# State products in four narrow column tiles, placed between the past products

## The chip, the cores and the metric

The kernel runs on one core of a Trainium2 chip. The metric is the time of one execution on the device, in microseconds (us): the median of three runs is 507.63 (507.57 to 507.75).

## The reference

An attention of the RWKV kind, followed by a feed-forward layer with a cosine gate. Batch 4, 8 heads, 768 steps, head size 48; the feed-forward layer goes from 384 to 2048 and back. All float32.

```
for t in range(S):
    cur = einsum('bhd,bhe->bhde', u * k_t, v_t)
    y_t = einsum('bhd,bhde->bhe', r_t, state + cur)
    state = w_t[..., None] * state + einsum('bhd,bhe->bhde', k_t, v_t)
x = y, heads side by side (3072 x 384)
h = x @ w_in;  g = h * cos(h);  out = g @ w_out
```

## The kernel before, in words

The 768 steps of a batch are cut into 6 chunks of 128 steps. With 4 batches there are 24 chunks, taken position by position: chunk j has batch j % 4 and position c = j // 4 in it. Two chunks make a block; blocks are numbered 0 to 11. The eight heads lie as four pairs p of two heads h; head h of a pair has its 48 rows from partition 64 x h.

**Attention of a chunk.** VectorE makes decay products by scans (tokens e and f) and multiplies them into r and k (tokens r and k). TensorE then makes, per block:
- the scores pa (token a, function `att_scores`), which VectorE puts into the tile asb under a mask (token P);
- the transposes pt of the decayed k (token t, `att_transpose`, L401), which a copy brings into the tile kn (token K; on VectorE except in the first three blocks, where ScalarE does it);
- the own products py (token o, `att_own`, L458 and L464): asb times v in tiles of 32 columns;
- the past products (token p, `att_past`): the carried state against r, first over all 112 rows (L486), then over 48 rows (L490), both added into py;
- the state products pst (token s, `att_state`, L423): kn times v, in tiles of 64 and 48 columns. The sums (token n, `summed`) add the decayed old state dd and give the new state of that batch; for position c = 0 ScalarE copies instead. Position 5 needs no transposes and no state products, so blocks 10 and 11 have none.

dd is made by token d from the batch's state, and is copied into the tile past for the next past products. py becomes xT, a high and a low part (token X), which the dense products read.

**Feed-forward.** Eight slots to a block, each with 256 columns of the hidden layer. `mm1` (L571, 18 products) gives ph. The gate follows as a chain: I rounds (ScalarE), S reduces (VectorE), N is the sine (ScalarE), M multiplies (VectorE), H casts to the high part (ScalarE), L makes the low part (POOL). `mm2` (L589, 12 products) of the slot two before uses the result.

**The order is written out by hand.** Each engine runs its instructions in program order. START is a list of tokens for the first part, up to the state products of block 2 (tokens s0, s1, s2). After it come rows of tokens, one per slot: FIRST for the eight slots of the first round, then PLAN for every later one. In both, a token such as `t+2` is for chunk 2i + 2 and `o+1` for block i + 1, where i is the block whose feed-forward runs. So the attention of block 3 stands in FIRST, that of blocks 4 to 11 in PLAN. Slot 2 holds the transposes and K, slot 4 the scores and P, slot 6 the own, past and state products, X and n. Slots 5 differ:

```
FIRST[5] = "mm1 I S f+4 N M mm2 H L r+4 load+6"
PLAN[5]  = "mm1 I S u+4 N M mm2 H L"
```

PSUM banks of the attention (pa, pt, py, pst) are given out in turn from four, once the start is over.

Of the kernel before, what the change touches and what calls it, by code (L numbers as in the profile page):

```python
# [10 lines left out]
F32 = mybir.dt.float32  # L11
# [8 lines left out]
ALU = mybir.AluOpType  # L20
# [3 lines left out]
HD = 48  # L24
NP = 4
R96 = 2 * HD
ROW = 64
R = ROW + HD
NCB = 6
W129 = NP * 129  # L30
BLK = 2
# [4 lines left out]
RING = 5  # L36
BY_HAND = "P"
MERGE = 1
BUFS = dict(tt=5, v=4, h=2, rr=7, gs=2, asb=4, sn=4, xT=2, kn=4, ee=2, dd=2, cd=2, rkt=2)
LEAST = 1e-15  # L40
W_SCALE = 2.0 ** 8
INV2PI = 1.0 / (2.0 * math.pi)
# [4 lines left out]
ALL_OF = 6  # L47
# [8 lines left out]
LEAD = 0  # L56
PLAN = ["mm1 I S k+3 N M mm2 H L f+3",
# [7 lines left out]
START = """  # L65
ld0 e0 f0 q0 ld1 D19 pc0 e1 q1 k0 D5 t0 raw2 cd0 f1 wg2 pc1 cd1 ld2 r0 k1 W0 K0 wl2 A1 r1 D5 t1 e2 wy2 a1 a0 v0 raw0 f2
# [12 lines left out]
"""  # L79
FIRST = ["lr+2 lr+3 load+4 load+5 lv+4 lv+5 mm1 e+2 e+3 k+2 k+3 I S f+2 N M mm2 H L r+2",  # L80
# [7 lines left out]
LAST = "mm1 I S N M", "mm1 I S N M mm2 h l", "mm2 h l"  # L88
CHECK = 12
# [2 lines left out]
             o="a lv", s="t d lv", p="o d")  # L92
# [3 lines left out]
def rwkv_cos_ffn(ctx: ExitStack, tc: tile.TileContext, tr, tn, tv, u, ut, wts, w, rkw, vst, us, xs, out):  # L96
    nc = tc.nc
    NG = tr.shape[0]
# [7 lines left out]
    cst = ctx.enter_context(tc.tile_pool(name="cst", bufs=1))  # L106
# [6 lines left out]
    def bank(kind, shape, name):  # L113

        tags = BANKS[stage[0]]
        turn[kind] += 1
        return ps.tile(shape, F32, tag=tags[kind][turn[kind] % len(tags[kind])], name=name)
# [3 lines left out]
    def buf(tag, shape, dtype, name=None, pool=sb):  # L121
        return pool.tile(shape, dtype, tag=tag, name=name or tag, bufs=BUFS.get(tag, 1))
    ident = cst.tile([C, C], F32, name="ident")
# [19 lines left out]
    past = [cst.tile([R, NP, R96], F32, name="past%d" % n) for n in range(BLK)]  # L143
    for n in range(BLK):
        nc.gpsimd.memset(past[n], 0.0)
    quarter = cst.tile([128, 1], F32, name="quarter")
    nc.vector.memset(quarter, math.pi / 2.0)
    nc.scalar.activation(cst.tile([128, 1], F32, name="first_sine"), quarter, AF.Sin)
# [18 lines left out]
    def copy(name, out, in_):  # L167
        (nc.scalar.copy if E[name] is nc.scalar else E[name].tensor_copy)(out=out, in_=in_)  # L168

    def low_part(name, out, full, high):  # L170
        E[name].tensor_tensor(out=out, in0=full, in1=high.bitcast(F32), op=ALU.subtract)  # L171
# [46 lines left out]
    NB = NG // NCB  # L218
    order = chunk_order(NG)
    SAME = NB // BLK  # L220
    atts, states, outs, xts, units, accs = {}, {}, {}, {}, {}, {}
    placed_at = {}
    atts_loaded = []

# [2 lines left out]
    def part(key, run):  # L227

        assert key not in parts, key
        parts[key] = run  # L230
# [108 lines left out]
    def in_order(a, x, p):  # L339

        return x if p < TURNED or a["j"] < ALL_OF else turn_back(x)

    def rows(h):

        return slice(ROW * h, ROW * h + HD)
# [63 lines left out]
    def head_cols(p, h, n):  # L409

        at = p * R96 + h * HD
        return slice(at, at + n)

    def att_state(i):

        two = [a for a in (atts[i * BLK + n] for n in range(BLK)) if a["c"] < NCB - 1]
        pst = bank("a", [C, BLK, NP, HD], "pst") if two else None
        for n, a in enumerate(two):
            for p in range(NP):
                for h in range(2):  # L420
                    m = ROW if h == 0 else HD
                    at = v_col(p, h)
                    nc.tensor.matmul(out=pst[ROW * h:ROW * h + m, n, p], lhsT=a["kn"][:, head_cols(p, h, m)],  # L423
                                     rhs=a["v"][:, at:at + HD], start=True, stop=True)

        def summed():
            for n, a in enumerate(two):
                sn = buf("sn", [R, NP, HD], F32)
                if a["c"] == 0:
                    nc.scalar.copy(out=sn, in_=pst[:R, n])  # L430
                else:
                    nc.vector.tensor_tensor(out=sn, in0=pst[:R, n], in1=a["dd"], op=ALU.add)
                states[a["b"]] = sn

        part(("n", i), summed)

    def v_col(p, h):

        return p * PAIR_W + h * (HD + 16)
# [39 lines left out]
    def att_past(i):  # L479

        py, at = outs.pop(i)
        two = [atts[i * BLK + n] for n in range(BLK)]
        if two[0]["c"] > 0:
            for n, a in enumerate(two):
                for p in range(NP):
                    nc.tensor.matmul(out=at(1, n, p), lhsT=a["past"][:, p, 32:64], rhs=in_order(a, a["r3"][:, p], p),  # L486
                                     start=False, stop=True, skip_group_check=True)
            for n, a in enumerate(two):
                for kt, p, h, q in LONG:
                    nc.tensor.matmul(out=at(kt, n, q), lhsT=a["past"][rows(h), p, 64 * h:64 * h + 32],  # L490
                                     rhs=in_order(a, a["r3"][rows(h), p], p), start=False, stop=True, skip_group_check=True)

        halves_of = {}

        def high(side):
            if side == 0:
                xts[i] = buf("xT", [128, 2, KT, BT], F32R)
            halves_of["x"] = xts[i].rearrange("p o k t -> p o (k t)").rearrange("p o (s n) -> p o s n", s=2)
            copy("xh", halves_of["x"][:, 0, side], py[side].rearrange("p k t -> p (k t)"))

        def low(side):
            low_part("x", halves_of["x"][:, 1, side], py[side].rearrange("p k t -> p (k t)"), halves_of["x"][:, 0, side])

        def less(side):
            nc.tensor.matmul(out=py[side].rearrange("p k t -> p (k t)"), lhsT=nident, rhs=halves_of["x"][:, 0, side], start=False, stop=True, skip_group_check=True)

        def taken(side):
            nc.scalar.copy(out=halves_of["x"][:, 1, side], in_=py[side].rearrange("p k t -> p (k t)"))

        for side in range(2):  # L510
            part(("xh", (i, side)), lambda side=side: high(side))
            part(("xl", (i, side)), lambda side=side: low(side))
            if i <= BLK:
                part(("xp", (i, side)), lambda side=side: less(side))
                part(("xa", (i, side)), lambda side=side: taken(side))
# [99 lines left out]
    for i in PAIR:  # L615
# [5 lines left out]
    n_checked = [0]  # L621
    steps = dict(load=None, lr=att_load_rk, lv=att_load_v, decay=att_decay, diag=att_diag, d=att_dstate,
                 a=att_scores, t=att_transpose, s=att_state, o=att_own, p=att_past, x=att_x)

    def att(j, n):

        whole = n in "osp"
        if not 0 <= j < (NBLK if whole else NG) or (j, n) in seen:
            return
        for m in ("decay" if n == "diag" and j < BY_PE else NEEDS.get(n, "")).split():  # L630
            for c in (range(j * BLK, (j + 1) * BLK) if whole and m not in "osp" else (j,)):
                att(c, m)
        i = j // BLK
        if n == "load":
            for m in "osp":
                att((j - BUFS["tt"]) // BLK, m)
        elif n == "t":
            att((j - BUFS["kn"]) // BLK, "s")
        elif n == "d" and j >= NB:
            att(i - SAME, "s")  # L640
            att((j - BUFS["dd"]) // BLK, "s")
            att(i - 1, "p")
        elif n == "lv":
            att((j - BUFS["v"]) // BLK, "o")
            att((j - BUFS["v"]) // BLK, "s")
        elif n == "x":
            att(i, "p")
        seen.add((j, n))
        if n == "load":
            att_load(j)  # L650
        else:
            steps[n](j if whole else atts[j])
# [122 lines left out]
    with tc.manual_schedule(engines={ET.PE, ET.DVE, ET.Activation, ET.Pool}):  # L775
# [6 lines left out]
        for t in range(up2, slots + LAG):  # L782
            n = t - up2
# [187 lines left out]
```

## Time and profile before

| what | us |
|---|---|
| median of the runs | 507.63 |
| the profiled execution | 509.25 |
| its span, first to last instruction | 507.5 |
| TensorE matmul busy | 501.5 (99%) |
| VectorE busy | 378.9 (75%) |
| ScalarE busy | 256.0 (50%) |
| POOL busy | 202.5 (40%) |

A row of the timeline gives the start, the time from the first start to the last end, engine, line, operation, and how many instructions were merged; what stands in brackets is the idle time before it and what ended it. A float32 product is recorded as two matmuls. The records overlap, so the price of a stretch is read from its start to the start of the next one.

### The profile page before, as it was taken

The page shows a single profiled execution, that of the slowest core. Times are in us where ns is not written, and L with a number is a line of the kernel's source. Part 1 is how long each engine was busy: PE and PEld are TensorE (multiplying, and loading weights), DVE is VectorE, ACT ScalarE, POOL GpSimd, SP SyncE. Part 2 cuts the span into 40 slices and gives each one's busy share as a digit, 9 for nine tenths or more (in the row PEclk, how much of TensorE's full clock was granted, in tenths as well). Part 3 has the DMA queues.
Part 4 walks back from the last instruction along what each step waited for, and adds up shares of the span by engine and source line. Part 5 has one row for each costly group of instructions (what it writes and reads, how often), then busy time and mean ns, then how long its engine had stood idle before and what let it go on. Part 6 is the DMA issues. An engine that isn't in the chain of part 4 may idle for free.

```text
span 507.5 us, 12744 instructions
## 1 busy us (share of the span) xinstructions
PE 501.5 (99%) x5334; PEld 487.5 (96%) x5334; DVE 378.9 (75%) x669; ACT 256.0 (50%) x440; POOL 202.5 (40%) x273
## 2 busy tenths in 40 slices
PE   8999999999999999999999999999999999999997
PEld 8899999999999999999999999999999999999997
DVE  7989999777969758848947946956966975587633
ACT  2769788525355444444445435435444544544543
POOL 3434546435445335334333524523533533423330
PEclk9979999999999999999999999999999999999999
DMA  8978550142052051051040132113105103013001
GB/s 270 416 292 286 228 227 2 63 162 96 34 193 63 1 193 63 1 194 52 13 172 36 51 113 83 63 53 141 63 4 192 62 3 125 33 56 132 32 3 34
DMA packets 17324, 54.59 MB, mean 108 GB/s; under 512 B 2032, under 2 KB 8688, under 8 KB 17264
## 3 DMA queue, kind: packets, MB, share of 16 engines
q1 hardware_dynamic: 17120, 53.64, 29.7%
q8 instruction: 43, 0.70, 0.6%
q14 instruction: 17, 0.14, 0.1%
q10 hardware_dynamic: 144, 0.10, 0.1%
HBM read 49.02 MB, written 4.72 MB: 106 GB/s over the span
## 4 chain that ended last, share of the span: by engine, by line
PE 95%; DMA 2%; SPq 1%; ACT 0%; issue 0%; DVE 0%; DVEq 0%; ACTq 0%
PE ph L571 41%; PE acc L589 40%; PE pa L378 3%; DMA raw<-wts 2%; PE py L458 2%; PE py L464 2%; PE pst L423 2%; PE pt L401 2%; PE py L490 1%; PE py L486 1%; PE pa L370 1%; PE pc L307 1%; SPq L244 1%; SPq L262 0%; SPq L177 0%
## 5 line engine op out<-in xcount | busy, mean ns | idle before, releaser
L171 POOL TENSOR_TENSOR gs<-rr,gs 128x256 fp32r<-128x256 f32 x188 | 148.6, 811 | 236.9 <-ACT gs L168 214.2
L571 PE MATMUL ph<-xT,w 128*128 128x256 f32 x1728 | 222.2, 283 | 0.2 <-DVE w L202 0.2
L571 PEld LDWEIGHTS ph<-xT,w 128*128 128x128 f32 x1728 | 214.2, 190 | 2.3 <-PE py L490 0.4
L589 PE MATMUL acc<-w,gs 128*128 128x384 f32 x1152 | 215.6, 337 | 0.0
L589 PEld LDWEIGHTS acc<-w,gs 128*128 128x128 f32 x1152 | 196.1, 188 | 0.3 <-issue 0.2
L537 DVE SCALAR_TENSOR_TENSOR rr<-rr,ph 128x512 f32<-128x512 int32 x96 | 65.5, 682 | 63.6 <-ACT rr L534 62.5
L550 ACT ACTIVATE rr<-rr,quarter 128x512 f32<-128x512 f32 x96 | 69.5, 724 | 79.9 <-DVE rr L537 79.7
L534 ACT ACTIVATE rr<-ph 128x512 int32<-128x512 f32 x96 | 57.3, 597 | 68.3 <-PE ph L571 67.8
L168 ACT CAST gs<-rr 128x512 fp32r<-128x512 f32 x88 | 54.6, 621 | 63.2 <-DVE rr L551 39.1
L551 DVE TENSOR_TENSOR rr<-rr,ph 128x512 f32<-128x512 f32 x96 | 65.5, 682 | 22.3 <-ACT rr L550 20.0
L331 POOL TENSOR_SCALAR_AFFINE_SELECT asb<-cd 128x512 f32<-128x512 f32 x48 | 40.8, 876 | 53.2 <-DVE cd L321 35.5
L392 DVE COPY_PREDICATED asb<-turned_mask,pa 64x128 f32<-64x128 uint8 (+1 forms) x108 | 33.6, 346 | 2.1 <-POOL asb L331 0.3
L279 DVE TENSOR_TENSOR_SCAN ee<-tt,one_e 112x516 f32<-112x516 f32 (+1 forms) x25 | 31.6, 1269 | 2.0 <-DMA tt<-tr 2.0
L285 DVE TENSOR_TENSOR_SCAN tt<-tt,inj 112x516 f32<-112x516 f32 x24 | 30.3, 1262 | 0.8
L171 DVE TENSOR_TENSOR xT<-py,xT 128x384 fp32r<-128x384 f32 x22 | 11.3, 551 | 21.4 <-ACT xT L168 21.4
L192 ACT ACTIVATE top<-raw 128x768 f16<-128x768 bf16 x16 | 17.5, 1091 | 2.7 <-DMA raw<-wts 2.7
L458 PE MATMUL py<-asb,v 128*32 128x128 f32 x384 | 17.4, 276 | 0.0
L200 DVE CUSTOM_DVE_ANT_0 h<-h,top 128x1536 uint16<-128x1536 uint16 x16 | 16.1, 1005 | 1.7 <-ACT top L192 0.9
L464 PE MATMUL py<-asb,v 128*32 128x128 f32 x384 | 17.1, 273 | 0.0
L168 ACT CAST xT<-py 128x384 fp32r<-128x384 f32 x24 | 10.3, 482 | 12.7 <-PE py L490 11.6
L168 ACT COPY past<-dd 48x192 f32<-48x192 f32 x40 | 14.0, 349 | 2.7 <-DVE dd L354 2.4
L378 PEld LDWEIGHTS pa<-tt 48*64 48x64 f32 x576 | 12.9, 133 | 2.2 <-issue 2.2
(89 smaller groups left out, 364.4 us busy)
## 6 DMA issues: line engine op xcount, KB each, us to landing
tt<-tr SPq DMA_DIRECT2D x22, 770.5 KB, 6.6
raw<-wts SPq DMA_DIRECT2D x16, 767.8 KB, 6.9
rk<-tn SPq DMA_DIRECT2D x18, 384.0 KB, 3.2
v<-tv SPq DMA_DIRECT2D x24, 224.0 KB, 4.7
ww<-w SPq DMA_DIRECT2D x6, 768.0 KB, 5.1
out<-ob SPq DMA_DIRECT2D x23, 192.0 KB, 2.0
tt<-tr SPq DMA_DIRECT2D x4, 256.0 KB, 4.0
tt<-tr SPq DMA_DIRECT2D x1, 258.5 KB, 4.3
```

The source lines that it names most:

```text
L168: (nc.scalar.copy if E[name] is nc.scalar else E[name].tensor_copy)(out=out, in_=in_)
L171: E[name].tensor_tensor(out=out, in0=full, in1=high.bitcast(F32), op=ALU.subtract)
L279: nc.vector.tensor_tensor_scan(out=ee[:, pairs].rearrange("p a t -> p (a t)")[:, ::-1], data0=wp[:, cols][:, ::-1], data1=one_e[:, pairs]. ...
L285: nc.vector.tensor_tensor_scan(out=wp[:, 0:W129], data0=wp[:, 0:W129], data1=inj.rearrange("p a t -> p (a t)"), initial=0.0, op0=ALU.mult, ...
L331: nc.gpsimd.affine_select(out=asb, in_=col.unsqueeze(2).to_broadcast([C, NP, C]), pattern=[[0, 4], [1, C]], compare_op=ALU.is_equal, fill= ...
L392: nc.vector.copy_predicated(*(which(x) for x in (a["asb", h], turned_mask, pa[h])))
L534: nc.scalar.activation(made["rr"].bitcast(I32), ph, AF.Copy, scale=INV2PI / W_SCALE, bias=0.25)
L537: nc.vector.scalar_tensor_tensor(out=made["rr"], in0=made["rr"].bitcast(I32), scalar=-2.0 * math.pi * W_SCALE, in1=ph, op0=ALU.mult, op1=A ...
L550: N=lambda: nc.scalar.activation(made["rr"], made["rr"], AF.Sin, scale=1.0 / W_SCALE, bias=quarter),
L551: M=lambda: nc.vector.tensor_tensor(out=made["rr"], in0=made["rr"], in1=ph, op=ALU.mult), H=high, L=low)
L571: nc.tensor.matmul(out=ph[:, fi], lhsT=wgt[u * FU + fi][:, 0, a, kt * 128:(kt + 1) * 128], rhs=xT[:, b, kt], start=n == 0, stop=n == 3 * K ...
L589: nc.tensor.matmul(out=accs[i][j][:, :DM], lhsT=gs[:, a, fi, j * C:(j + 1) * C], rhs=wgt[u * FU + fi][:, 1, b], start=u == 0 and fi == 0 a ...
```

## The change

The products of a state are cut from one of 64 or 48 columns into one of 32 and one of 16, at the partitions 0, 32, 64 and 96. The sums go by head, two per chunk instead of one, and the states live in four fixed tiles (one per batch) instead of a ring of four buffers; the rows between the heads are set to zero once. From block 3 on the state products are issued between the two kinds of past products, and the transposes and the copies K stand in slot 6, ahead of the own products, instead of slot 2. START keeps its tokens.

```diff
-BUFS = dict(tt=5, v=4, h=2, rr=7, gs=2, asb=4, sn=4, xT=2, kn=4, ee=2, dd=2, cd=2, rkt=2)
+BUFS = dict(tt=5, v=4, h=2, rr=7, gs=2, asb=4, xT=2, kn=4, ee=2, dd=2, cd=2, rkt=2)
 PLAN = [...
-        "t+2 t+3 load+6 mm1 K+2 K+3 e+4 I S k+4 N M mm2 H L f+4",
+        "load+6 mm1 e+4 I S k+4 N M mm2 H L f+4",
...
-        "o+1 p+1 s+1 mm1 load+7 lv+6 lv+7 X+1 n+1 I S c+4 N M mm2 H L d+4",
+        "t+2 t+3 K+2 K+3 o+1 p+1 s+1 mm1 load+7 lv+6 lv+7 X+1 n+1 I S c+4 N M mm2 H L d+4",
 FIRST = [...
-         "mm1 t+2 t+3 I S K+2 K+3 N M mm2 H L m+2 u+2 c+2 d+2",
+         "mm1 I S N M mm2 H L m+2 u+2 c+2 d+2",
...
-         "o+1 p+1 s+1 mm1 load+7 lv+6 lv+7 X+1 n+1 I S N M mm2 H L m+4 u+4 c+4 d+4",
+         "t+2 t+3 K+2 K+3 o+1 p+1 s+1 mm1 load+7 lv+6 lv+7 X+1 n+1 I S N M mm2 H L m+4 u+4 c+4 d+4",
...
+    all_states = cst.tile([R, NG // NCB, NP, HD], F32, name="all_states")
+    nc.gpsimd.memset(all_states[32:ROW], 0.0)
...
-    atts, states, outs, xts, units, accs = {}, {}, {}, {}, {}, {}
+    atts, outs, xts, units, accs = {}, {}, {}, {}, {}
+    states = [all_states[:, b] for b in range(NB)]
...
             for p in range(NP):
-                for h in range(2):
-                    m = ROW if h == 0 else HD
-                    at = v_col(p, h)
-                    nc.tensor.matmul(out=pst[ROW * h:ROW * h + m, n, p], lhsT=a["kn"][:, head_cols(p, h, m)],
-                                     rhs=a["v"][:, at:at + HD], start=True, stop=True)
+                for first, m in ((0, 32), (32, HD - 32)):
+                    for h in range(2):
+                        at = v_col(p, h)
+                        to = ROW * h + first
+                        nc.tensor.matmul(out=pst[to:to + m, n, p], lhsT=a["kn"][:, head_cols(p, h, HD)][:, first:first + m],
+                                         rhs=a["v"][:, at:at + HD], start=True, stop=True)
 
         def summed():
             for n, a in enumerate(two):
-                sn = buf("sn", [R, NP, HD], F32)
-                if a["c"] == 0:
-                    nc.scalar.copy(out=sn, in_=pst[:R, n])
-                else:
-                    nc.vector.tensor_tensor(out=sn, in0=pst[:R, n], in1=a["dd"], op=ALU.add)
-                states[a["b"]] = sn
+                sn = states[a["b"]]
+                for h in range(2):
+                    if a["c"] == 0:
+                        nc.scalar.copy(out=sn[rows(h)], in_=pst[rows(h), n])
+                    else:
+                        nc.vector.tensor_tensor(out=sn[rows(h)], in0=pst[rows(h), n], in1=a["dd"][rows(h)], op=ALU.add)
...
                     nc.tensor.matmul(out=at(1, n, p), lhsT=a["past"][:, p, 32:64], rhs=in_order(a, a["r3"][:, p], p),
                                      start=False, stop=True, skip_group_check=True)
+            if i * BLK >= ALL_OF:
+                att(i, "s")
             for n, a in enumerate(two):
                 for kt, p, h, q in LONG:
```

## Rows read from the trace of the kernel before

**Rows 1.** The page's chain that ended last, shares of the span by engine.

```profile
PE 95%; DMA 2%; SPq 1%; ACT 0%; issue 0%; DVE 0%; DVEq 0%; ACTq 0%
```

**Rows 2.** Timeline of TensorE over block 5: start, us, engine, line, count.

```profile
216.14 0.64 PE L458 MATMUL py<-asb,v 128*32 128x128 f32 x16
...
217.91 0.62 PE L486 MATMUL py<-tt,past 112*32 112x128 f32 x16
218.46 0.67 PE L490 MATMUL py<-tt,past 48*32 48x128 f32 x32
219.06 1.13 PE L423 MATMUL pst<-v,kn 128*64 128x48 f32 x32
220.12 2.37 PE L571 MATMUL ph<-xT,w 128*128 128x256 f32 x18
...
236.97 0.93 PE L401 MATMUL pt<-ident,tt 112*128 112x112 f32 x8
237.67 2.35 PE L571 MATMUL ph<-xT,w 128*128 128x256 f32 x18
239.85 2.25 PE L589 MATMUL acc<-w,gs 128*128 128x384 f32 x12
```

**Rows 3.** The same timeline at block 10, which has no state products.

```profile
418.51 0.67 PE L490 MATMUL py<-tt,past 48*32 48x128 f32 x32
419.11 2.36 PE L571 MATMUL ph<-xT,w 128*128 128x256 f32 x18
```

**Rows 4.** Timeline of VectorE at block 5: S and M of slot 5.

```profile
214.79 0.69 DVE L537 SCALAR_TENSOR_TENSOR rr<-rr,ph 128x512 f32<-128x512 int32 x1 [1.32 <-ACT rr L534]
...
216.27 0.69 DVE L551 TENSOR_TENSOR rr<-rr,ph 128x512 f32<-128x512 f32 x1 [0.15 <-ACT rr L550]
```

**Rows 5.** Timeline of TensorE at block 3.

```profile
131.53 2.26 PE L571 MATMUL ph<-xT,w 128*128 128x256 f32 x18
133.63 2.25 PE L589 MATMUL acc<-w,gs 128*128 128x384 f32 x12
135.81 0.64 PE L458 MATMUL py<-asb,v 128*32 128x128 f32 x16
...
139.79 2.37 PE L571 MATMUL ph<-xT,w 128*128 128x256 f32 x18
```

**Rows 6.** Timeline of VectorE from block 2's sums to block 3's r+4.

```profile
108.12 0.62 DVE L432 TENSOR_TENSOR sn<-pst,dd 112x192 f32<-112x192 f32 x2 [0.60 <-PE pst L423]
...
120.91 1.01 DVE L168 COPY kn<-pt 128x384 f32<-128x384 f32 x2
...
136.78 0.69 DVE L537 SCALAR_TENSOR_TENSOR rr<-rr,ph 128x512 f32<-128x512 int32 x1 [0.59 <-ACT rr L534]
...
139.69 0.41 DVE L298 TENSOR_TENSOR tt<-tt 112x256 f32<-112x256 f32 x1
```

**Rows 7.** Timeline of ScalarE there: the sine of slot 2, the cast of slot 4.

```profile
121.02 0.73 ACT L550 ACTIVATE rr<-rr,quarter 128x512 f32<-128x512 f32 x1 [0.82 <-DVE rr L537]
...
135.63 0.62 ACT L168 CAST gs<-rr 128x512 fp32r<-128x512 f32 x1 [1.07 <-DVE rr L551]
```

**Rows 8.** Stretches: us, busy PE PEld DVE ACT POOL, clock, DMA share, GB/s.

```profile
25.16:32.00 6.84, 6.84 (x35) 6.84 (x35) 6.67 (x9) 4.48 (x11) 3.93 (x3) 0.50 0.91 369
...
504.00:506.40 2.40, 0.09 (x1) 0.00 (x0) 0.36 (x1) 0.33 (x1) 0.00 (x0) 1.00 0.51 167
506.40:507.50 1.10, 0.00 (x0) 0.00 (x0) 0.00 (x0) 0.00 (x0) 0.00 (x0) 0.52 0.03 7
```

**Rows 9.** Timeline of TensorE in the start, the first 18 dense products.

```profile
26.20 4.19 PE L571 MATMUL ph<-xT,w 128*128 128x256 f32 x18
```

**Rows 10.** Timeline of TensorE later in the start, a wait for weights.

```profile
64.95 1.66 PE L571 MATMUL ph<-xT,w 128*128 128x256 f32 x12 [0.16 <-DVE w L202]
```

**Rows 11.** Timeline of ScalarE behind block 1's copies of the states.

```profile
37.82 0.86 ACT L168 CAST xT<-py 128x384 fp32r<-128x384 f32 x2 [1.12 <-PE py L458]
```

**Rows 12.** Group by line, POOL's memsets: count, busy us, mean ns, idle before.

```profile
L151 POOL MEMSET top<- 128x768 int32 x2 | 1.4, 738 | 0.0
```

## The prediction

> **What bounds the kernel now.** I read the chain that ended last first: TensorE is 95% of it [rows 1]. So a change pays only in TensorE's order of work, or costs where it makes TensorE wait. Next I read TensorE's timeline over one block of the steady part, start to start. Block 5's attention runs from 216.14 to 220.12: own products 1.77 us, first past products (112 rows) 0.55, second past products (48 rows) 0.60, state products 1.06; then the dense products go on [rows 2]. Nothing waits there, so these differences are prices. The other blocks from 4 to 9 repeat them.
>
> Then I read the same stretch of block 10, which has no state products: the 48-row products again take 0.60 before the dense ones follow [rows 3]. So the state products cost exactly their 1.06, and leaving the 48-row products costs the same whatever comes next.
>
> Last I read who is busy where the moved transposes will stand. In block 5 VectorE has waited 1.32 us for the rounding that starts slot 5, so it follows TensorE [rows 4]. Around block 3, the first block after the hand-written start, VectorE is late: at 139.69, well after block 3's own products began at 135.81, it still works on the last operation of slot 5 [rows 5, 6].
>
> **Part 1: the state products, blocks 4 to 9.** Before, 16 products per block are recorded as 32. They run in two column tiles, 64 and 48 wide, so 16 rounds of two: 1.06/16 = 0.066 us a round with the change of tile shape in it. After, 64 are recorded in four column tiles, so 16 rounds of four, in the shape of the own products (128 rows by 32 columns).
>
> What is a round of four with 48 moving columns? Own products: 64 records, 16 rounds of four with 128 moving columns, 1.77/16 = 0.110. If a round goes by its moving columns it is 0.110 x 48/128 = 0.041, the low end. If it goes by its four records and four weight loads it stays 0.110, the high end. The 48-row products, 32 records in 0.60 with a change of shape in it, speak for the low one: under 0.019 a record, against 0.028 in the own products. I take 0.045.
>
> What is a change of shape? The 112-row products are four rounds of four in the own products' shape: 4 x 0.110 = 0.44. They take 0.55 up to the 48-row ones: 0.11 for the change.
>
> Sum per block, from the first 112-row product to the dense work: before 0.55 + 0.60 + 1.06 = 2.21 [rows 2]. After: 0.44, then the states without a change, 16 x 0.045 = 0.72, the change 0.11, the 48-row products 0.60: 1.87. Gain 0.34; ends a gain of 0.40 and a loss of 0.70. This part breaks even at 0.066 a round.
>
> [...]
>
> **Part 2: the transposes.** In slot 2 they cost 0.70, and the 18 dense products behind them take 2.18 instead of 2.10 [rows 2, 5]: 0.78. In front of the own products they cost about the same 0.78: the change of shape behind the dense products (0.09: the twelve take 2.18 up to the own products [rows 5]) merely moves behind them. I take 0, ends -0.09 and +0.09 a block.
>
> **Part 3: the copies K behind them (PSUM to kn), on VectorE.** They now stand at the head of slot 6, behind all of slot 5 on that engine. The state products need them 0.78 + 1.77 + 0.44 = 3.0 us after the transposes' start.
> In blocks 4 to 9 slot 5's last VectorE operation ends at 216.27 + 0.69 = 216.96 [rows 4]; transposes would start 0.09 before 216.14, at 216.05. Two copies take 1.01 [rows 6]: done at 217.97, needed from 219.0. Hidden, with 1.1 us to spare. Behind K on VectorE wait the low halves of xT, the sums and slot 6's reduction; they wait for the 48-row products or the next dense ones anyway.
>
> Block 3 is different: its slot 5 also holds the forward scan and two decay products r+4. I work out both sides in the time of before.
> TensorE: block 2's state products, the same 32 records, shrink from 1.06 to 0.83 (0.72 + 0.11), -0.23; the transposes leave slot 2, -0.78. They start at 135.81 - 0.09 - 1.01 = 134.71 instead, own products at 135.6, and the state products are due at 137.8.
> VectorE: from block 2's sums on it runs without a break that is TensorE's. Those sums are two operations in 0.62 [rows 6], a step of 0.27; the change makes them four, +0.54, and they start 0.21 earlier: +0.33. Taking K out of slot 2 gives nearly nothing back: the copies end at 120.91 + 1.01 = 121.92 and the sine that the next operation needs at 121.02 + 0.73 = 121.75 [rows 6, 7]. I take -0.05 for it, ends -1.0 and 0. Its waits further on are not TensorE's: the 0.59 at 136.78 is for a rounding, queued on ScalarE behind a cast that had itself waited 1.07 for VectorE [rows 6, 7]. So the last r+4 ends at 139.69 + 0.41 + 0.29 = 140.4, the first copy at 140.9, the second at 141.4.
> TensorE waits from 137.8 to 140.9, 3.1 us. The second chunk's half starts at 141.4: 8 x 0.045 + 0.11 + 0.60 later, at 142.47, the dense ones. Before, they start at 139.79 [rows 5]: +2.68 us in all, block 2's gain and the transposes' move included. Ends: 1.7, if VectorE does win a full 1.0, and 3.0.
>
> **Part 4: TensorE's clock.** [...] At half speed the 18 dense products take 4.19 against 2.26 [rows 5, 9]. The spell lasted 6.84, so it cost 3.4. That is the high end, 0 the low end; I take the middle, 1.7, since here dense work follows at once while part of that spell had thin work in it.
>
> **Part 5: the rest, at nothing.** Block 0 and 1 stand in the start; block 1's gain could be 0.32, as it also loses a change of shape. TensorE waits later for weights from VectorE [rows 10], which is nearly always busy there, so I take 0, ends -0.3 and 0. Their sums become four ScalarE copies instead of two (+0.54 at the same step); ScalarE waits 1.12 for the own products right behind [rows 11], which hides them; without that cover 0.5. The new memset of 768 elements costs POOL about 0.74 [rows 12] before any tile is picked; without cover 0.7. In blocks 4 to 9 two more sums cost VectorE 0.54, in front of a reduction that waits for dense products; without cover 0.5 a block, but the product that needs it comes two slots later. SP: no DMA moves; the loads of k, r, w free at the 48-row products, some 1.4 us later within slot 6, and are used a block later.
>
> **The sum.** +2.68 (block 3), 6 x -0.34 = -2.04 (blocks 4 to 9), +1.7 (clock): +2.3. The profiled execution took 509.25 (span 507.5, 1.75 around it): 511.6 by that. The median of the runs is 507.63, 1.62 lower; with the same difference 509.9.
>
> **Rivals.**
> (a) VectorE is in time in block 3. Then nothing waits and the clock stays: -0.23 - 0.34 - 2.04 = -2.6, 505.0. For it: VectorE is relieved of 1.01 us in slot 2, and block 3 is one of seven. Against: it decides at copies done by 137.8, and the rows put them 3.1 us later; no operation between is that long. 0.11.
> (b) The wait comes, the clock doesn't fall: 507.63 + 0.64 = 508.3. For it: short waits, as [rows 10], left the clock alone. [...] 0.17.
> (c) The clock stays down as long as in the start: 3.4 instead of 1.7, 511.6. 0.18.
> (d) Records and weight loads, not columns, set the round: 0.110 as in the own products. Blocks 2 and 4 to 9 each lose 16 x 0.065 = 1.04 against my sum, block 3 half of it: 509.9 + 7.8 = 517.7. For it: every product of this shape so far goes at 0.110 a round. Against: the 48-row products at 0.019 a record. 0.04. [...]
> My forecast, wait and a shorter slow spell: 0.46. The remaining 0.04 is for a first wait elsewhere.
>
> **How the numbers follow.** My own case reaches from 508.9 to 511.0 (a round at 0.041 to 0.055, the spell 1.2 to 2.4). The range goes down to 507.5 to hold (b), up to 512.0 to hold (c); outside are (a), (d) and half of the rest. About 0.2%, 1.0 us, is what a measurement of this kernel tells from no change: 506.6 to 508.65. Faster: (a) with a little of the rest, 0.12. Within: most of (b), 0.15. Slower: 0.73.
>
> **What would show it.** Steady blocks: the own products, 112-row, state and 48-row products in this order, 112-row to dense 1.87, state round 0.045. Block 3: TensorE idle some 3 us before its state products, released by the copy into kn on VectorE, r+4 just before it. Granted clock 0.5 in a stretch right behind. If block 3's state products start without a wait, the prediction is wrong by its main term; if the clock stays at 1.0 there, by its last.

## The result, and the profile after

The changed kernel takes 510.68 us (median of seven runs, 509.56 to 513.16) where the kernel before took 507.76 beside it: ratio 1.0052 [1.0033, 1.0072], half a per cent slower. Its profiled execution took 511.16 (span 509.4). Forecast were 509.9, range 507.5 to 512.0.

The chain that ended last, shares of the span by engine. It answers to [rows 1], where TensorE had 95%:

```profile
PE 84%; DVE 6%; DMA 3%; ACT 2%; SPq 1%; issue 1%; POOL 1%; ACTq 0%; DVEq 0%
```

Where the chain leaves TensorE is seen in its pieces in order of time (start, us, what), from block 2 to block 3:

```profile
104.83 0.86 PE pst L427 x48
105.72 0.35 DVE all_states L437
106.08 0.36 DVE all_states L437
106.46 0.35 DVE all_states L437
106.82 0.36 DVE all_states L437
107.20 2.36 DVE ee L282 x2
...
118.22 0.75 POOL gs L173
...
138.82 0.48 DVE kn L170
139.34 0.67 PE pst L427 x19
```

For 34 us, from block 2's sums to the first copy into kn, the end is set by VectorE and its partners, and TensorE lives on what it has in hand. It runs out in block 3. Timeline of TensorE there, answering to [rows 5]:

```profile
133.38 0.65 PE L462 MATMUL py<-asb,v 128*32 128x128 f32 x16
...
135.15 0.62 PE L490 MATMUL py<-tt,past 112*32 112x128 f32 x16
139.34 1.49 PE L427 MATMUL pst<-v,kn 128*32 128x48 f32 x64 [3.57 <-DVE kn L170]
140.76 1.11 PE L496 MATMUL py<-tt,past 48*32 48x128 f32 x32
141.80 3.79 PE L577 MATMUL ph<-xT,w 128*128 128x256 f32 x18
```

The state products stand 4.19 behind the start of the 112-row products, where block 5 needs 0.44 for the same step, and everything behind them runs at half pace: 18 dense products in 3.6 instead of 2.2. The stretches there (us, busy PE PEld DVE ACT POOL, granted clock, DMA share, GB/s), answering to [rows 8]:

```profile
135.50:138.12 2.62, 0.27 (x12) 0.00 (x0) 2.58 (x5) 0.72 (x1) 2.05 (x3) 1.00 0.00 0
138.12:139.30 1.18, 0.00 (x0) 0.00 (x0) 1.18 (x5) 0.62 (x1) 0.34 (x1) 0.50 0.00 0
139.30:144.94 5.64, 5.60 (x110) 5.10 (x111) 2.80 (x7) 0.86 (x2) 1.07 (x2) 0.50 0.60 162
144.94:150.00 5.06, 5.06 (x38) 5.06 (x38) 2.88 (x6) 1.95 (x3) 0.76 (x1) 1.00 0.57 230
```

TensorE does nothing, the granted clock falls from 1.00 to 0.50 inside the wait and is back at 1.00 from 144.94 on. VectorE is busy for 2.58 + 1.18 of the 3.80 us up to 139.30. Its timeline, answering to [rows 6]:

```profile
105.72 1.46 DVE L437 TENSOR_TENSOR all_states<-pst,dd 48x192 f32<-48x192 f32 x4 [0.37 <-PE pst L427]
107.20 2.36 DVE L282 TENSOR_TENSOR_SCAN ee<-tt,one_e 112x516 f32<-112x516 f32 x2
...
119.09 0.69 DVE L543 SCALAR_TENSOR_TENSOR rr<-rr,ph 128x512 f32<-128x512 int32 x1 [0.99 <-POOL gs L173]
...
138.40 0.41 DVE L301 TENSOR_TENSOR tt<-tt 112x256 f32<-112x256 f32 x1
138.74 1.01 DVE L170 COPY kn<-pt 128x384 f32<-128x384 f32 x2
```

The copies K follow the last r+4 directly.

A block that does not wait gains. TensorE in block 5, answering to [rows 2]:

```profile
220.91 0.62 PE L490 MATMUL py<-tt,past 112*32 112x128 f32 x16
221.35 0.87 PE L427 MATMUL pst<-v,kn 128*32 128x48 f32 x64
222.15 0.67 PE L496 MATMUL py<-tt,past 48*32 48x128 f32 x32
222.75 1.44 PE L577 MATMUL ph<-xT,w 128*128 128x256 f32 x10
```

From the 112-row products to the dense ones it is 222.75 - 220.91 = 1.84; it was 2.21 [rows 2]. For the whole account I measure from the own products of one block to those of the next, from block 2 on. The start ahead of block 2 took 96.6 to 99.9 in these profiles and does not follow the edits: the place-only kernel below has the same instructions in it as the kernel before, and reached block 2 at 98.31 against 99.64. It goes with the half-speed spell that stands in it, from about 25 us on: the three profiles in which that spell lasts 6.8 us (before, transposes only, tiles and place) reach block 2 at 99.6 to 99.9, the eight in which it lasts 3.4 us or is missing at 96.6 to 98.3.

| kernel | 2 to 3 | 3 to 4 | 4 to 10 | 10 to end | 2 to end |
|---|---|---|---|---|---|
| before | 36.17 | 40.17 | 240.21 | 91.36 | 407.91 |
| after | 35.91 | 46.01 | 238.72 | 91.35 | 411.98 |
| after, in its second profile | 35.91 | 45.11 | 238.42 | 93.62 | 413.06 |
| block 3's transposes back in slot 2 | 35.94 | 40.28 | 238.42 | 91.35 | 406.00 |
| wait filled with idle products | 35.91 | 43.64 | 238.79 | 91.55 | 409.89 |
| tiles only | 35.94 | 39.93 | 238.97 | 91.35 | 406.19 |
| place only | 36.18 | 40.17 | 240.23 | 91.34 | 407.92 |
| transposes only | 36.16 | 43.54 | 240.16 | 91.35 | 411.21 |
| decays later | 35.91 | 42.84 | 238.29 | 91.39 | 408.43 |
| tiles and place | 35.94 | 39.79 | 238.79 | 91.35 | 405.87 |
| sums by head | 35.91 | 45.79 | 238.81 | 91.35 | 411.86 |

One interval loses 5.84, six gain 1.49 together, one 0.26: +4.07 from block 2 on, of which this execution's start, with the shorter spell, gave 2.2 back.

### The profile page after: what moved, and what is told of

Same layout as the page of the kernel before. It is cut to its first block, busy times and chain, and to the rows that moved or that the text cites. A ratio compares the mean times of both kernels' runs of the same rounds, so it can differ in the third digit from the quotient of the medians.

```text
span 509.4 us, 13401 instructions
## 1 busy us (share of the span) xinstructions
PE 498.6 (98%) x5654; PEld 485.2 (95%) x5654; DVE 386.9 (76%) x685; ACT 257.1 (50%) x444; POOL 206.5 (41%) x274
## 4 chain that ended last, share of the span: by engine, by line
PE 84%; DVE 6%; DMA 3%; ACT 2%; SPq 1%; issue 1%; POOL 1%; ACTq 0%; DVEq 0%
PE acc L595 36%; PE ph L577 36%; DMA raw<-wts 3%; PE pa L381 2%; PE py L462 2%; PE py L468 2%; PE py L496 1%; PE pst L427 1%; PE pt L404 1%; DVE rr L557 1%; DVE rr L543 1%; PE py L490 1%; DVE tt L288 1%; DVE ee L282 1%; SPq L247 1%
## 5 line engine op out<-in xcount | busy, mean ns | idle before, releaser
L173 POOL TENSOR_TENSOR gs<-rr,gs 128x256 fp32r<-128x256 f32 x188 | 154.4, 842 | 231.8 <-ACT gs L170 210.3
L334 POOL TENSOR_SCALAR_AFFINE_SELECT asb<-cd 128x512 f32<-128x512 f32 x48 | 37.2, 800 | 55.7 <-DVE cd L324 38.5
```

The costliest lines, as they stand in the source:

```text
L334: nc.gpsimd.affine_select(out=asb, in_=col.unsqueeze(2).to_broadcast([C, NP, C]), pattern=[[0, 4], [1, C]], compare_op=ALU.is_equal, fill= ...
```

## The experiments

**1. The first round's transposes put back.** The changed kernel with the tokens of FIRST alone as before; PLAN keeps them in slot 6.

```
- FIRST[2]  "mm1 I S N M mm2 H L m+2 ..."
+ FIRST[2]  "mm1 t+2 t+3 I S K+2 K+3 N M mm2 H L m+2 ..."
- FIRST[6]  "t+2 t+3 K+2 K+3 o+1 p+1 s+1 mm1 ..."
+ FIRST[6]  "o+1 p+1 s+1 mm1 ..."
```

> The changed kernel with the transposes and copies of block 3 back in slot 2 (the first round's row only); all else as changed. Theory (the loss is the wait for the copy into kn in block 3 and the slow clock behind it, while every other block gains 0.38): no wait in block 3, which then gains like the others; 507.76 - 0.26 (block 2) - 7 x 0.38, plus up to 0.9 if the two short waits for issue in blocks 6 and 7 stay: 504.8 to 505.7. Rival (the narrow tiles themselves cost, through issue waits or the sums on VectorE): still above 507.8.

Measured: 505.42 (505.01 to 506.48), ratio 0.9945 [0.9932, 0.9959], as expected. TensorE in block 3:

```profile
135.10 0.62 PE L490 MATMUL py<-tt,past 112*32 112x128 f32 x16
135.54 0.86 PE L427 MATMUL pst<-v,kn 128*32 128x48 f32 x64
...
136.94 2.37 PE L577 MATMUL ph<-xT,w 128*128 128x256 f32 x18
```

No wait, no slow dense products, and the interval from block 3 to 4 is 40.28. Moving the transposes of one round accounts for the whole loss: 411.98 - 406.00 = 6.0 in the profiles, 5.3 between the medians of the two sets of runs. The 0.5 that the interval has over the later 39.76 are breaks in the dense products near 156, with no releaser in the profile. This kernel is faster than both; against the kernel before it gains half a per cent.

**2. The wait filled.** The changed kernel with 14 idle products of 128 x 128 (28 records) in block 3, between the 112-row products and the state products. They write a tile that nobody reads.

```
+ if i == 3:
+     ...
+     filled = ps.tile([C, C], F32, ...)
+     for again in range(14):
+         nc.tensor.matmul(out=filled, lhsT=ident, rhs=ident, start=True, stop=True)
  att(i, "s")
```

> The changed kernel with 14 idle 128x128 products of the identity (28 records, some 3.1 us) put in block 3 between the 112-row products and the state products, where TensorE waits 3.7 us; nothing reads them. Theory (the wait costs by itself and again by the clock): the wait stays as long, the clock stays at 1.0 around it, and the time is that of the wait alone: 509.4, with little scatter. Rival (the clock is a by-product that costs nothing): 510.7 as the changed kernel. Second rival (TensorE was waiting for room, not for the copy): the idle products add their 3 us.

Measured: 509.80 (508.54 to 511.06), ratio 1.0028 [1.0011, 1.0046]. TensorE, and then its stretches:

```profile
135.89 3.39 PE L497 MATMUL filled<-ident 128*128 128x128 f32 x28
139.51 1.00 PE L427 MATMUL pst<-v,kn 128*32 128x48 f32 x64 [0.23 <-DVE kn L170]
...
141.04 2.37 PE L582 MATMUL ph<-xT,w 128*128 128x256 f32 x18
```

```profile
136.00:139.50 3.50, 3.28 (x28) 3.09 (x28) 3.47 (x8) 1.34 (x2) 2.09 (x3) 1.00 0.03 7
139.50:145.00 5.50, 5.49 (x125) 5.16 (x126) 3.45 (x8) 1.66 (x4) 1.05 (x2) 1.00 0.59 167
```

The state products start 5.94 behind the own ones, as in the changed kernel (5.96): the idle products delay nothing. But the clock stays at 1.00 and the 18 dense products take 2.2 again. So wait and clock come apart: 43.64 - 39.76 (the step of a later block) = 3.88 is the wait, 46.01 - 43.64 = 2.37 the clock's fall; 1.47 in the changed kernel's second profile. Rival (b), a wait without a fall, is what this kernel does and the changed one does not. That rests on the profiles: the medians, with ratios of 1.0028 and 1.0052 whose intervals overlap, would not show it, and the little scatter that was expected did not come (2.5 us from the lowest run to the highest).

**3. The tiles only, 4. the place only, 5. the transposes only.** Experiment 3 is the changed kernel with FIRST and PLAN as before and the state products behind the 48-row products. Experiment 4 is the kernel before with the two lines

```
+ if i * BLK >= ALL_OF:
+     att(i, "s")
```

Experiment 5 is the kernel before (wide tiles, two sums, state products last) with the four rows of FIRST and PLAN as changed.

> The kernel before with the narrow tiles, the four state tiles and the sums by head alone: transposes in slot 2, state products behind the 48-row products. Theory: the 64 records take 0.80 from their start to the dense products instead of 1.06, in blocks 2 to 9: -0.26 x 8 = -2.1, so 505.7. Rival (the gain comes from the place between the past products, not from the tiles): 507.8.

> The kernel before with the state products, in their wide tiles, issued between the 112-row and the 48-row products; transposes in slot 2. Theory: as many changes of tile shape as before, so no change: 507.8 within 0.3. Rival (the place alone brings the gain): -0.1 x 7 or more, 507.0 or less.

> The kernel before with the transposes and copies moved to slot 6 in both tables, state products wide and behind the 48-row products. Theory (block 3's copies stand behind all of slot 5 on VectorE): the state products of block 3 are due 0.6 later and VectorE's sums in block 2 are not longer, so TensorE waits some 1.9 us there instead of 3.7; from block 3's own products to block 4's 42.1 instead of 40.17, more if the clock falls; total about 509.7. Rival (the wait needs the narrow tiles or the place between the past products): no wait, 507.9.

Measured: tiles 505.10 (504.6 to 506.0), ratio 0.9939 [0.9927, 0.9952]; place 507.96, ratio 0.9997 [0.9983, 1.0011]; transposes 510.85 (508.59 to 513.08), ratio 1.0044 [1.0024, 1.0064]. The place did nothing, as expected; the tiles gained more than expected. By its ratio the tiles' gain is some 3.1 us, of which the profile shows 1.72 from block 2 on; where the rest lies is not shown. The tiles, at block 3, take 0.80 from their start to that of the dense products, the wide ones 1.06 [rows 2]:

```profile
135.46 0.87 PE L427 MATMUL pst<-v,kn 128*32 128x48 f32 x64
136.26 2.37 PE L575 MATMUL ph<-xT,w 128*128 128x256 f32 x18
```

The place moves the wide tiles' 1.06 without changing it, in block 5:

```profile
217.14 1.13 PE L423 MATMUL pst<-v,kn 128*64 128x48 f32 x32
218.20 0.67 PE L492 MATMUL py<-tt,past 48*32 48x128 f32 x32
```

The transposes alone bring the wait and the fall (TensorE in block 3, then the stretch behind the wait):

```profile
140.50 1.73 PE L423 MATMUL pst<-v,kn 128*64 128x48 f32 x32 [1.78 <-DVE kn L168]
142.16 3.30 PE L571 MATMUL ph<-xT,w 128*128 128x256 f32 x18
```

```profile
140.50:144.30 3.80, 3.80 (x42) 3.71 (x43) 1.96 (x5) 0.29 (x1) 1.02 (x2) 0.55 0.85 288
```

The wait came as forecast, the interval not: 43.54 against the 42.1 that left the clock out; a fall behind 1.78 of idle time I had not counted. VectorE's slot 2 in this kernel starts with a wait for ScalarE, as in the kernel before, and in block 3 its copy K stands 40.33 behind block 2's own products:

```profile
120.25 0.69 DVE L537 SCALAR_TENSOR_TENSOR rr<-rr,ph 128x512 f32<-128x512 int32 x1 [0.64 <-ACT rr L534]
...
139.90 1.01 DVE L168 COPY kn<-pt 128x384 f32<-128x384 f32 x2
```

In the changed kernel that copy stands at 138.74 - 97.46 = 41.28. So the narrow tiles, with their four sums, make VectorE 0.95 later (the account below splits this into the sums and a second wait): the two halves of the change add to each other's cost.

**6. The decays later.** In the changed kernel the forward scan and the r+4 products leave slot 5 of the first round for slot 7, out of K's way.

```
- FIRST[5]  "mm1 I S f+4 N M mm2 H L r+4 load+6"
+ FIRST[5]  "mm1 I S N M mm2 H L load+6"
- FIRST[7]  "mm1 I S m+5 N M mm2 H L e+5 lr+6"
+ FIRST[7]  "mm1 I S m+5 f+4 N M mm2 H L r+4 e+5 lr+6"
```

> The changed kernel with the forward scan and the decay products f+4 and r+4 moved from slot 5 to slot 7 of the first round, so that 2.1 us less stand ahead of the copies on VectorE in block 3. Theory: the wait falls by as much, from 3.7 to 1.6; the clock may stay up; block 3 to block 4 takes 41.4 instead of 46.0, total about 507.3. Rival (the copies are late for another reason, such as TensorE's transposes or a bank of PSUM): the wait stays at 3.7.

Measured: 509.31 (507.25 to 510.14, and one run of 608.26 that the ratio leaves out), ratio 1.0014 [0.9998, 1.0031], not told from the kernel before. The expectation held in its direction only: the wait is 2.42, not 1.6. TensorE, its stretches, then VectorE:

```profile
138.27 1.00 PE L427 MATMUL pst<-v,kn 128*32 128x48 f32 x64 [2.42 <-DVE kn L170]
```

```profile
136.00:138.30 2.30, 0.03 (x4) 0.04 (x8) 1.51 (x4) 1.17 (x2) 0.55 (x1) 1.00 0.00 0
138.30:145.00 6.70, 6.70 (x134) 6.38 (x135) 4.10 (x10) 2.35 (x5) 1.42 (x2) 1.00 0.65 215
```

```profile
137.05 0.69 DVE L557 TENSOR_TENSOR rr<-rr,ph 128x512 f32<-128x512 f32 x1 [0.79 <-ACT rr L556]
137.66 1.02 DVE L170 COPY kn<-pt 128x384 f32<-128x384 f32 x2
```

I had taken the scan's 1.25 off the path. It had hidden the sine that the next multiply needs; without it VectorE waits 0.79 for that. In this execution the clock stayed at 1.00 through the 2.42 of idle time, though in experiment 5 it fell behind 1.78. It need not be typical: its mean granted clock is 0.997, and seven of the other eleven runs have 0.992 or 0.993.

**7. Tiles and place.** The changed kernel with FIRST and PLAN as before: everything but the move of the transposes.

> The kernel before with the narrow tiles and the place between the past products, transposes and copies in slot 2 in both tables. Theory: no wait in block 3, 0.38 less per block from block 3 on: 39.8 from own products to own products, total about 504.5, plus up to 0.9 if waits for issue come. Rival (the place brings nothing beside the tiles): 39.9 a block and 505.1 as with the tiles alone.

Measured: 505.35 (504.35 to 507.48), ratio 0.9941 [0.9919, 0.9963]. Its undisturbed block takes 39.79, tiles only 39.92, before 40.17: the tiles give 0.25, the place between the past products 0.12 more, but only with the narrow tiles (experiment 4). The medians of the two, 505.35 and 505.10, can't be told apart; from block 2 on this profile is 0.32 shorter. Some of what the place gives is lost again in a break: the interval from block 7 to 8 is 40.59, 0.80 over the others, where the tiles alone have a break of 0.22. TensorE in block 7:

```profile
298.05 0.63 PE L496 MATMUL py<-tt,past 48*32 48x128 f32 x21
299.04 0.44 PE L496 MATMUL py<-tt,past 48*32 48x128 f32 x11 [0.36 <-issue]
```

**8. The changed kernel again**, beside experiments 5 to 7.

> The changed kernel once more, on the same chip as the three above. Theory: the wait in block 3 is there in every execution, 3.6 to 3.8 us, and the waits for issue in blocks 6 and 7 too; the clock behind it may or may not fall: 509.4 without, some 2.8 more with. Rival (the wait was an accident of one execution): 505 to 506.

Measured: 512.75 (510.57 to 515.95), ratio 1.0085 [1.0055, 1.0115]. The wait on kn is 3.54; the half-speed spell begins 0.85 behind its end and lasts 3.4 instead of 6.8:

```profile
139.75 1.02 PE L427 MATMUL pst<-v,kn 128*32 128x48 f32 x64 [3.54 <-DVE kn L170]
```

```profile
140.60:144.00 3.40, 3.40 (x58) 2.93 (x45) 1.63 (x4) 0.86 (x2) 0.19 (x1) 0.50 0.67 161
```

The wait came again at the same length, so the rival is out; the spell kept neither its place nor its length. The median lies 4.5 above the 508.23 of the kernel before in this set. The last interval is 2.3 longer in the profile, as the last outputs landed later, which the change does not touch.

**9. The sums by head.** In the changed kernel a block's sums alternate between rows 0 to 47 and 64 to 111. Here both chunks' upper rows come first:

```
- for n, a in enumerate(two):
-     for h in range(2):
+ for h in range(2):
+     for n, a in enumerate(two):
```

> The changed kernel, with the four sums of a block in another order: both chunks' rows 0 to 47 first, then both chunks' rows 64 to 111. Theory: a VectorE operation that starts at other partitions than the one before it does not overlap with it, so in the changed kernel each of the four sums takes a step of 0.37 us where the two sums of before took 0.27. In the new order only every second sum changes its rows: steps of 0.27, 0.37, 0.27, 0.37, the four last 1.27 instead of 1.48, the scans behind them start 0.2 earlier after block 2's own products (9.5 instead of 9.74), and TensorE's wait in block 3 is 3.3 instead of 3.5. Rival: sums of 48 rows take a step of 0.37 whatever stands before them (a property of their shape, or of two halves of one tile): steps 0.37 throughout, scans at 9.74, wait 3.5. The time itself changes by 0.2 at most and cannot tell.

Measured, in one execution (511.55 us): VectorE, then TensorE in block 3.

```profile
106.24 1.26 DVE L437 TENSOR_TENSOR all_states<-pst,dd 48x192 f32<-48x192 f32 x4 [0.36 <-PE pst L427]
107.52 2.36 DVE L282 TENSOR_TENSOR_SCAN ee<-tt,one_e 112x516 f32<-112x516 f32 x2
```

```profile
139.63 1.49 PE L427 MATMUL pst<-v,kn 128*32 128x48 f32 x64 [3.34 <-DVE kn L170]
```

The single sums start 0.275, 0.353 and 0.281 after one another; in the changed kernel 0.362, 0.375 and 0.363. The scans stand 107.52 - 97.99 = 9.53 behind block 2's own products, the wait is 0.2 shorter. The clock fell again: it was 0.50 from 139.60 to 142.00. A step costs 0.26 to 0.28 when the rows stay and 0.35 or more when they change. Operations of the same 48 rows take either step, so their shape does not set it, and the rival is out.

## Why the prediction was right, step by step

**Part 1, the state products: right, a little small.** 2.21 fell to 1.84, where 1.87 was forecast. The 64 records take 222.15 - 221.35 = 0.80 with the change of shape behind them, forecast 16 x 0.045 + 0.11 = 0.83; the 112-row products ahead of them take 0.44, as forecast without one. The change of shape saved by the place is 0.12 (experiment 7 against 3), taken as 0.11. The 64 records in 0.80 are 12.5 ns each, in four column tiles. Rival (d), a round at 0.110, falls by the same 0.80: less the 0.11 of the change of shape it is 0.043 a round.

**Part 2, the transposes: right.** The steady block gains 0.40 (40.17 to 39.77), of which the stretch of part 1 has 0.37: about 0.03 for the move, forecast at 0 with ends of 0.09.

**Part 3, the copies K: right in place and order, too small.** The wait stands in block 3, is released by the copy into kn, with r+4 right ahead of it; blocks 4 to 9 hide K (in block 5 VectorE's two copies start at 219.15 and take 1.02, so they end at 220.17, needed at 221.35). So rival (a) is out. Its length is 139.34 - (135.15 + 0.44) = 3.75 from the moment that the products were due, forecast 3.1. TensorE was as predicted: 38.13 behind block 2's own products when it ran out, forecast 137.8 - 99.64 = 38.16. VectorE was 0.89 later at the end of r+4 than before, not 0.29. Two terms were mis-sized:
- The sums. Priced at 0.54 more, at the step of 0.27 that two sums had [rows 6]; measured are 107.20 - 105.72 = 1.48 for four against 0.54 for two, 0.94 more. Experiment 9 shows why: here a sum at other partitions than the one before it starts 0.35 or more after it, one at the same partitions 0.28 or less. The sums start 0.22 earlier, as forecast, and 0.12 more is given back on the way, so that slot 0's reduction is 0.60 later.
- A new wait, not in the forecast. Slot 2's reduction waits 0.99 for POOL, where before it waited 0.64 for ScalarE: the delay grows from 0.61 to 0.97. It is there in every traced kernel with four sums (also in those with K in slot 2), and in none with two (experiments 4 and 5). Every kernel with four sums also has the fixed state tiles and their memset, and no run parts these. Why POOL's low halves come to matter at this point stays open.

**Part 4, the clock: right, with a weak reason.** It fell, and cost 2.37 in one profile and 1.47 in the other; no run shows the 1.7 itself, which was only the middle between 0 and the 3.4 that the 6.84 us at 0.50 in the start cost [rows 8]. Rival (c)'s full spell of 6.8 did come in the first (and in experiment 9), but cost less than 3.4: 1.2 of it lay in the wait. The spell in the start did not follow a long wait: TensorE was busy for 2.72 of the 3.16 us ahead of it, from 22.00 to 25.16, and throughout it; only the fall at the end of the kernel stands behind little work, 0.09 in 2.40 [rows 8]. Nor are those 2.40 us a bound: the clock fell behind 1.78 in experiment 5 and stayed at 1.00 behind 2.42 in experiment 6. The short wait that (b) names, 0.16 [rows 10], left it at 1.00 from 64.00 to 67.00.

**Part 5: right but for one thing.** ScalarE's four copies are hidden (it still waits 0.24 for the own products behind them), and so is the memset (0.73 of POOL; block 0's own products start at 19.03, before at 19.67). The sums' cost in blocks 4 to 9 is hidden too: three of these six intervals are 39.76 to 39.78. Not foreseen were the breaks in the 48-row products: 0.17 behind block 6's and 0.69 behind block 7's, which take the six blocks' gain from 2.35 to 1.49 (forecast 2.04). In the waits of the weight loads for these products (us in total, times, longest) four stand in the changed kernel, the longest of 0.6; in the kernel before there are ten, none over 0.2:

```profile
PEld py L496 <- issue: 1.2, 4, 0.6
```

```profile
PEld py L490 <- issue: 2.0, 10, 0.2
```

**The sum.** From block 2 on it is +4.07 in the profile against +2.3. Block 3 with block 2's gain, taken without the clock (43.64 - 40.17 - 0.26 = 3.21, forecast 2.68), makes 0.53 of the difference, the clock 0.67, and blocks 4 to 9 make 0.55 (breaks of 0.86, less 0.31 that the blocks gain beyond the forecast). All three terms erred the same way. The medians lie 2.92 apart, so the forecast of 2.3 was nearer to these than its terms deserve, and that was luck: the forecast left out the start, whose spell differs from execution to execution. In the second set of runs, experiment 8, the same kernel's median of 512.75 lies above the range.

## What to carry to other kernels

A step that is moved takes its copies with it: what counts is where they land in the queue of the engine that makes them, and the first block after a special start has another queue than the steady ones, so it is priced by itself. Splitting a small operation in two can cost its engine more than twice the time when the halves lie on other partitions: here 1.48 against 0.54. On TensorE a wait can have a second price in the granted clock: here 1.5 to 2.4 us on top of waits of 1.8 to 3.6, in four of the five profiles in which TensorE waited idle for the copies. The repair is to give the moved step its old place in that one round (505.4) or not to move it at all (505.1 and 505.35); the runs can't tell these three apart.

## What the runs showed of the hardware that was not expected

- VectorE's sums did not overlap where the start partition changed: steps of 0.35 to 0.39 us where 0.26 to 0.28 were paid on equal ones, for operations of 0.34 to 0.36 (changed kernel and experiment 9).
- The granted clock fell behind 1.78 us of idle TensorE (experiment 5, 0.55 in the mean from 140.50 to 144.30) and with waits of 3.3 to 3.6 (the changed kernel twice and experiment 9, to 0.50), and stayed at 1.00 behind 2.42 (experiment 6): in these five executions the length of the wait alone does not tell. In the changed kernel it fell once inside the wait and once 0.85 us behind its end.
- Breaks of 0.2 to 0.8 us a block in TensorE's stream, released by nothing that the profile shows. From block 3 on they stand in all eight profiles with narrow state products and in none of the three with wide ones (before, experiments 4 and 5). Most lie in the 48-row products of block 7 (experiments 6 and 7) or of blocks 6 and 7 (the changed kernel, experiments 1 and 9); with the same products last there is one of 0.22 (experiment 3), and some lie in dense products (near 156 in experiment 1, 159 in experiment 6, 381 in experiment 2). With 28 records more ahead of them, in experiment 2, they stand in blocks 8 and 9 instead. Their cause stays open.
